# Delta rule and slot mixture: each head in its own 32 partitions, 32x32 diagonal products, layouts by VectorE block transposes

## Chip, core and metric

The kernel runs on one core of one Trainium2 chip. The metric is the device time of one execution in microseconds (us), the median of several runs. Everything is f32. The engines named here are TensorE (PE, with its weight loads as PEld), VectorE (DVE), ScalarE (ACT), GpSimd (POOL) and SyncE (SP, which only issues DMAs).

## The reference

Two blocks, one behind the other. The first is a delta rule over 768 tokens for 4 batch rows and 8 heads of 48 features; the second is a soft mixture of 8 experts with 4 slots each over the 3072 rows of 384 features that come out.

```python
# q, k, v: (4, 8, 768, 48); beta: (4, 8, 768)
k_n = k / (np.linalg.norm(k, axis=-1, keepdims=True) + 1e-06)
for t in range(S):
    y[:, :, t] = q_t @ state
    v_old = k_t @ state
    state = state + beta_t * outer(k_t, v_t - v_old)      # per batch row and head, 48 x 48
x = y.transpose(0, 2, 1, 3).reshape(3072, 384)
logits = x @ phi                                          # 3072 x 32 slots
d = softmax over the tokens; slot_input = d.T @ x         # 32 x 384
slot_out[e] = relu(slot_input[e] @ w1[e]) @ w2[e]         # 8 experts, 384 -> 1024 -> 384
out = softmax over the slots (logits) @ slot_out
```

## The kernel before

**Tiling.** Tokens are taken in 24 chunks of 32, and four chunks make a group (6 groups). A *unit* is one batch row b and one half g of the heads (4 heads), so that there are 8 units; in a unit, head h of the four and token t stand on partition 32 h + t. All 8 units of a chunk lie side by side in the free dimension.

**What does not depend on the state** is made for one group ahead. `norm` scales the keys (squares and scaling on POOL, the sum and a root with a correction step on DVE and ACT). `prep` brings K and Q of a chunk into `KQ` with features on partitions, by eight 128x128 PE transposes (L215) and two ACT copies (L218); then it forms K K^T and Q K^T by head, 48 rows by 32 columns (L230). ACT copies the first into `Lc` (L232). DVE spreads the second, masked, into `AT` (L233), where the four heads of a unit stand on the diagonal of a 128x128 matrix with zeros between them. `invert` forms the inverse of I + L of all four chunks at once: `Lc` goes to DRAM (`ld`, L250) and back as `lb` (L251), so that each partition holds one 32x32 block; POOL multiplies by beta (L252); then 31 elimination steps of two DVE instructions each (L264, L267) follow; the result goes to DRAM (`td`, L272). `near` fetches from there the inverse of the next chunk into the diagonal blocks of `TTs` (L282), and spreads the keys over the heads as `KX` on POOL (L291).

**One chunk** (`chunk`), with the state S: psR = K S (L310), R = V - psR on DVE (L314), psW = T R with a 128x128 matrix for each unit (L324), U = beta psW on DVE (L329), psS = K^T U (L340), S = S + psS on DVE (L345), psY = Q S + AT U (L354, and L359 with 128x128 matrices), and Y by ACT (L362). It goes by two halves of the batch rows, `hf`.

**Routing** (`route`) of a group follows one group later: logits (L379, L385), the two softmaxes, and the slots' inputs (L443, L453 on POOL, L458).

**The experts** (L532 on) come at the end, w1 as the stationary operand (L557), w2 as the moving one (L568), and then the output (L588).

**Order.** The code hands out steps of the work ahead and of the routing between the parts of a chunk (`Fill`, `merge`). A scheduler then orders each engine's queue by when it expects operands, so that the order on an engine is not the order of the code. Each engine takes its queue strictly in that order. An f32 product is two records of MATMUL and two of LDWEIGHTS in the trace (L340: 736 calls, x1472); a PE transpose is one of each.

Of the kernel before, what the change touches and what calls it, by code (L numbers as in the profile page):

```python
# [16 lines left out]
def kernel(  # L17
# [30 lines left out]
    DP = 64  # L48
# [5 lines left out]
    assert G == 2 and B == 4 and GC * U == C and Dm == H * D and NSL == C  # L54
# [5 lines left out]
    dp = ctx.enter_context(tc.tile_pool(name="dp", bufs=2, space=bass.MemoryType.DRAM))  # L60
# [8 lines left out]
    Ks = [io.tile([P, GC, U, DP], F32, name=f"Ks{i}", bufs=1) for i in range(2)]  # L69
    Qs = io.tile([P, GC, U, DP], F32, name="Qs", bufs=1)  # L70
    Vt = {}

    def load(src, dst, n, eng):
        for c in range(GC):
            for h in range(4):
                s0 = (n * GC + c) * C
                eng.dma_start(  # L77
                    out=dst[C * h:C * h + C, c, :, 0:D],
                    in_=src.rearrange("b (g h) s d -> h s (b g) d", h=4)[h, s0:s0 + C])

# [542 lines left out]
```

## Time and profile before

| | before |
|---|---|
| median of 3 runs | 921.85 us (921.1 to 922.2) |
| the profiled execution: its span | 919.5 us |
| TensorE busy | 679.9 us (74%) in 8324 matmuls |
| VectorE busy | 299.4 us (33%) |
| GpSimd busy | 192.9 us (21%) |
| ScalarE busy | 101.3 us (11%) |
| instructions | 19108 |

The span runs from the first to the last instruction of one execution; the run's time is 2.35 us longer. The busy share is an average over parts that differ: a start until the first inverse is there, six groups of chunks, the routing of the last group, and the experts. How each of them is bounded is read from the views below: the windows give busy time by stretch, the timeline gives single instructions with the idle time before them and what ended it, and the groups by line give counts and mean durations.

### The profile page before, as it was taken

The page shows a single profiled execution, that of the slowest core. Times are in us where ns is not written, and L with a number is a line of the kernel's source. Part 1 is how long each engine was busy: PE and PEld are TensorE (multiplying, and loading weights), DVE is VectorE, ACT ScalarE, POOL GpSimd, SP SyncE. Part 2 cuts the span into 40 slices and gives each one's busy share as a digit, 9 for nine tenths or more (in the row PEclk, how much of TensorE's full clock was granted, in tenths as well). Part 3 has the DMA queues.
Part 4 walks back from the last instruction along what each step waited for, and adds up shares of the span by engine and source line. Part 5 has one row for each costly group of instructions (what it writes and reads, how often), then busy time and mean ns, then how long its engine had stood idle before and what let it go on. Part 6 is the DMA issues. An engine that isn't in the chain of part 4 may idle for free.

```text
span 919.5 us, 19108 instructions
## 1 busy us (share of the span) xinstructions
PE 679.9 (74%) x8324; PEld 565.6 (62%) x8324; DVE 299.4 (33%) x816; ACT 101.3 (11%) x223; POOL 192.9 (21%) x347
## 2 busy tenths in 40 slices
PE   1706569069990799807998069996499799999998
PEld 1504569058880688706888058885398696765754
DVE  3267112942139421394213942226421100000011
ACT  0303000021120211102111021111000110000001
POOL 7231213131251213412134111351210200000000
PEclk9999999999995555755557555565555567667765
DMA  6240763023310242102321021000100099990013
GB/s 118 37 85 26 133 115 72 1 52 55 75 20 0 58 70 55 20 0 58 69 55 19 0 58 32 25 2 0 35 13 1 1 266 211 237 231 16 1 60 146
DMA packets 148019, 58.12 MB, mean 63 GB/s; under 512 B 131968, under 2 KB 143328, under 8 KB 147936
## 3 DMA queue, kind: packets, MB, share of 16 engines
q1 hardware_dynamic: 141888, 55.87, 27.9%
q10 hardware_dynamic: 5664, 0.94, 0.6%
q8 instruction: 65, 1.06, 0.5%
q0 software_dynamic: 384, 0.10, 0.1%
q14 instruction: 18, 0.15, 0.1%
HBM read 45.86 MB, written 11.01 MB: 62 GB/s over the span
## 4 chain that ended last, share of the span: by engine, by line
PE 64%; DVE 17%; DMA 6%; POOL 4%; SPq 3%; ACT 3%; issue 2%; ACTq 0%; DVEq 0%; POOLq 0%
PE ph L557 9%; PE psW L324 8%; PE psY L359 7%; DVE pr L264 7%; PE pso L568 6%; PE psS L340 6%; DVE tt L267 6%; PE pt L215 5%; PE pt L385 5%; PE pt L458 3%; PE pout L588 3%; PE psR L310 2%; PE pt L230 2%; PE psY L354 2%; PE pt L379 2%; SPq L77 2%
## 5 line engine op out<-in xcount | busy, mean ns | idle before, releaser
L215 PE MATMUL pt<-ident,Ks 128*128 128x128 f32 x96 | 42.1, 438 | 167.9 <-POOL Ks L199 158.7
L291 POOL TENSOR_TENSOR KX<-Ks,hm 128x192 f32<-128x192 f32 x184 | 91.0, 531 | 354.0 <-PE psS L340 264.4
L215 PEld LDWEIGHTS pt<-ident,Ks 128*128 128x128 f32 x96 | 20.8, 216 | 173.9 <-POOL Ks L199 159.6
L324 PE MATMUL psW<-R,TT 128*128 128x48 f32 x384 | 86.6, 396 | 34.4 <-DMA TT<-td 31.2
L324 PEld LDWEIGHTS psW<-R,TT 128*128 128x128 f32 x384 | 81.1, 311 | 39.4 <-DMA TT<-td 19.1
L557 PEld LDWEIGHTS ph<-sacc,w1t 96*128 96x128 f32 x512 | 87.8, 272 | 3.8 <-issue 3.8
L557 PE MATMUL ph<-sacc,w1t 96*128 96x4 f32 x512 | 88.1, 310 | 0.0
L359 PE MATMUL psY<-U,AT 128*128 128x48 f32 x384 | 83.9, 393 | 0.0
L264 DVE TENSOR_TENSOR pr<-tt,lb 128x31 f32<-128x31 f32 (+15 forms) x186 | 76.7, 413 | 16.2 <-POOL lb L252 11.0
L359 PEld LDWEIGHTS psY<-U,AT 128*128 128x128 f32 x384 | 78.2, 306 | 3.4
L267 DVE TENSOR_TENSOR tt<-tt,pr 128x31 f32<-128x31 f32 (+15 forms) x186 | 73.3, 394 | 5.2
L340 PE MATMUL psS<-U,KX 128*48 128x48 f32 x1472 | 69.8, 271 | 0.0
L340 PEld LDWEIGHTS psS<-U,KX 128*48 128x48 f32 x1472 | 60.8, 181 | 6.3 <-issue 1.7
L568 PE MATMUL pso<-w2t,hx 128*32 128x384 f32 x128 | 58.5, 627 | 1.7 <-DVE hx L561 1.7
L329 DVE TENSOR_TENSOR U<-psW,bta 128x192 f32<-128x192 f32 x48 | 17.2, 358 | 113.4 <-PE psW L324 113.4
L345 DVE TENSOR_TENSOR S<-S,psS 112x384 f32<-112x384 f32 x46 | 25.5, 554 | 87.6 <-PE psS L340 87.3
L233 DVE TENSOR_TENSOR AT<-pt,bdm 128x512 f32<-128x512 f32 x48 | 31.9, 688 | 62.1 <-ACT Lc L232 59.0
L385 PE MATMUL pt<-phi,yT 96*128 96x32 f32 x192 | 45.1, 398 | 6.0 <-ACT yT L381 5.1
L230 PE MATMUL pt<-KQ 48*32 48x64 f32 x1536 | 47.5, 310 | 1.9
L385 PEld LDWEIGHTS pt<-phi,yT 96*128 96x128 f32 x192 | 42.0, 323 | 10.5 <-ACT yT L381 9.1
L561 DVE TENSOR_SCALAR hx<-ph 128x32 f32<-128x32 f32 x8 | 1.5, 192 | 141.0 <-PE ph L557 141.0
L354 PE MATMUL psY<-S,KQ 48*32 48x48 f32 x1536 | 46.1, 265 | 0.1
(107 smaller groups left out, 698.9 us busy)
## 6 DMA issues: line engine op xcount, KB each, us to landing
w1t<-in_moe_w_dram SPq DMA_DIRECT2D x16, 768.0 KB
w2t<-in_moe_w_dram SPq DMA_DIRECT2D x8, 1536.0 KB
Ks<-in_k_dram SPq DMA_DIRECT2D x96, 48.0 KB
V<-in_v_dram SPq DMA_DIRECT2D x96, 48.0 KB
out_dram<-ob SPq DMA_DIRECT2D x24, 192.0 KB
Qs<-in_q_dram SPq DMA_DIRECT2D x80, 48.0 KB
ld<-Lc SPq DMA_DIRECT2D x24, 128.0 KB
lb<-ld SPq DMA_DIRECT2D x6, 512.0 KB
```

The lines of the kernel that those rows point to most:

```text
L215: nc.tensor.transpose(tp[:, i, a, :], src[:, c, b * G:(b + 1) * G, :].rearrange("p g d -> p (g d)"), ident)
L230: nc.tensor.matmul(pg[rh, b], lhsT=KQ[cc][r, b, 0, rh], rhs=KQ[cc][r, b, :, rh], start=True, stop=True, skip_group_check=True)
L264: nc.vector.tensor_tensor(prv, tt[:, 0:m, j:j + 1].broadcast_to([P, m, w]), lb[:, j, j + 1:C].unsqueeze(1).broadcast_to([P, m, w]), op=ALU ...
L267: nc.vector.tensor_tensor(tt[:, 0:m, j + 1:C], tt[:, 0:m, j + 1:C], prv, op=ALU.subtract)
L291: nc.gpsimd.tensor_tensor(KX[cc][:, g, b], kn[:, b].unsqueeze(1).broadcast_to([P, 4, D]), hm.unsqueeze(2).broadcast_to([P, 4, D]), op=ALU. ...
L324: nc.tensor.matmul(pw[:, i, g, :], lhsT=T[:, (2 * hf + i) * G + g].rearrange("p h t -> p (h t)"), rhs=Rs[hf][:, i, g, :], start=True, stop ...
L340: nc.tensor.matmul(psS[DP * g:DP * g + D, i, h, :], lhsT=kx[:, g, 2 * hf + i, h, :], rhs=Us[hf][:, i, g, :], start=True, stop=True, skip_g ...
L354: nc.tensor.matmul(py[C * h:C * h + C, b, :], lhsT=kq[r, b, 1, C * h:C * h + C], rhs=old[b // 2][r, b % 2, h, :], start=(b == 0), stop=Fal ...
L359: nc.tensor.matmul(py[:, b, :], lhsT=at[:, g, b].rearrange("p h t -> p (h t)"), rhs=Us[b // 2][:, b % 2, g, :], start=False, stop=True, sk ...
L385: nc.tensor.matmul(pl, lhsT=yT[:, h].rearrange("p c t -> p (c t)"), rhs=phi[:, h, :], start=(h == 0), stop=(h == 3))
L557: nc.tensor.matmul(st["ph"][:, t, :], lhsT=w1t[e][:, h, t * P:(t + 1) * P], rhs=sacc[:, h, sl], start=(h == 0), stop=(h == 3))
L568: nc.tensor.matmul(pso, lhsT=hx[:, e, t, :], rhs=w2t[e][:, t, :], start=(e == 0 and t == 0), stop=(e == E - 1 and t == NFC - 1))
```

## The change

Each head now keeps to its own 32 partitions in all products. The 48 features of a head are split into 32 and 16 (`a` = 0, 1), and each product with K, Q or the state is two accumulating products, whose operand rows, weights and output all lie in the 32 partitions of head h. So T, `AT` and K need no zeros between the heads: `TT`, `AT` and the keys are used as they are, as 32x32 blocks at the places (h, h) of the array.

- `KQ` comes from DVE block transposes (32x32 in place), four instructions a chunk, instead of eight PE transposes and two ACT copies. `Lc` to `lb` and `tt` to `TT` are DVE block transposes too; `ld`, `td`, `near`, `TTs` and `KX` are gone, and so are beta's second copy `bta` and its DMAs.
- beta goes into the inverse by one POOL multiply (`back`), so U is a plain ACT copy. The state is summed in PSUM over all chunks (`start` only at the first), so S is an ACT copy of it, where a DVE addition stood.
- K has three buffers and Q two (two and one before), and a group's loads are issued at the start of a group two ahead. The work ahead is handed out in the first chunk of a group (`prep`) and in the three others (`invert` and routing, a third each).

The code for the experts and the routing's arithmetic stay as they are.

```diff
-    Ks = [io.tile([P, GC, U, DP], F32, name=f"Ks{i}", bufs=1) for i in range(2)]
-    Qs = io.tile([P, GC, U, DP], F32, name="Qs", bufs=1)
+    Ks = [io.tile([P, W * D + DX], F32, name=f"Ks{i}", bufs=1) for i in range(3)]
+    Qs = [io.tile([P, W * D + DX], F32, name=f"Qs{i}", bufs=1) for i in range(2)]
...
+    def rows(h, a=0):
+        return slice(C * h, C * h + (C if a == 0 else D - C))
+    def feats(a):
+        return slice(0, C) if a == 0 else slice(C, D)
...
-        def transposes(bh):
...
-                    nc.tensor.transpose(
-                        tp[:, i, a, :],
-                        src[:, c, b * G:(b + 1) * G, :].rearrange("p g d -> p (g d)"), ident)
-            nc.scalar.activation(KQ[cc][:, 2 * bh:2 * bh + 2], tp, ACT.Copy)
+        def transposes(a):
...
+            for i, t in enumerate((Ks[n % 3], Qs[n % 2])):
+                o = c * U * D + C * a
+                src = t[:, o:o + U * D].rearrange("p (u d) -> p u d", d=D)[:, :, 0:C]
+                nc.vector.transpose(KQ[cc][:, :, a, i, :], src)
...
+            for i in range(UH):
+                for a in range(2):
+                    for h in range(4):
+                        kq = KQ[cc][rows(h, a), hf * UH + i, a]
+                        nc.tensor.matmul(pg[rows(h), i], lhsT=kq[:, 0, :], rhs=kq,
+                                         start=(a == 0), stop=(a == 1), skip_group_check=True)
...
-                AT[cc][:, g], pg[:, :, 1, :].unsqueeze(2).broadcast_to([P, B, 4, C]),
-                bdm.unsqueeze(1).broadcast_to([P, B, 4, C]), op=ALU.mult)
+                AT[cc][:, hf * UH:hf * UH + UH], pg[:, :, 1, :],
+                upper.unsqueeze(1).broadcast_to([P, UH, C]), op=ALU.mult)
...
-                nc.sync.dma_start(out=ld[r].rearrange("u s t -> s u t"), in_=lc[r])
-            nc.sync.dma_start(out=lb, in_=ld)
+            nc.vector.transpose(lb, Lc.pop(n).rearrange("p w t -> p t w"))
...
-        def store():
-            TTb[n] = dp.tile([P, C, C], F32, name="td", tag="td")
-            nc.sync.dma_start(out=TTb[n], in_=st["tt"])
...
+        def back():
+            tt = st["tt"]
+            nc.gpsimd.tensor_tensor(tt, tt, bb[:, n].unsqueeze(2).broadcast_to([P, C, C]),
+                                    op=ALU.mult)
+            TT[n] = wk.tile([P, W, C], F32, name="TT", tag="TT")
+            nc.vector.transpose(TT[n].rearrange("p w i -> p i w"), tt)
...
+        def residual(hf):
...
+            for i in range(UH):
+                for a in range(2):
+                    for h in range(4):
+                        nc.tensor.matmul(pr[rows(h), i, :], lhsT=kq[rows(h, a), hf * UH + i, a, 0],
+                                         rhs=old[hf][rows(h, a), a, i, :],
+                                         start=(a == 0), stop=(a == 1), skip_group_check=True)
+            Rs[hf] = wk.tile([P, UH, D], F32, name="R", tag=f"R{hf}", bufs=1)
+            nc.vector.tensor_tensor(Rs[hf], v_, pr, op=ALU.subtract)
+        def update(hf):
...
+                    nc.tensor.matmul(pw[rows(h), i, :], lhsT=T[rows(h), w0 + hf * UH + i, :],
+                                     rhs=Rs[hf][rows(h), i, :],
...
+            nc.scalar.activation(Us[hf], pw, ACT.Copy)
+        def state(hf):
+            for a in range(2):
+                for i in range(UH):
+                    for h in range(4):
+                        nc.tensor.matmul(psS[hf][rows(h, a), a, i, :],
+                                         lhsT=Kf[rows(h), w0 + hf * UH + i, feats(a)],
+                                         rhs=Us[hf][rows(h), i, :],
+                                         start=(cc == 0 and a == 0 and i == 0), stop=True,
...
+            nc.scalar.activation(St[hf], psS[hf], ACT.Copy)
...
+        for i in range(U):
+            for h in range(4):
+                nc.tensor.matmul(py[rows(h), i, :], lhsT=at[rows(h), i, :],
+                                 rhs=Us[i // UH][rows(h), i % UH, :],
...
-    NF = 5
+    NF = 4
...
-        cut_i, cut_r = len(inv) // 2, len(routing) // 2
+        cut_i, cut_r = len(inv) // 3, len(routing) // 3
+        if n + 2 < NG:
+            load_k(n + 2)
+            load_q(n + 2)
```

GpSimd's queue between two groups, before: `sq` and the scaling are `norm` of the group two ahead, `db` is routing, and `lb` opens the elimination.

```order
L399 TENSOR_TENSOR Call<-el,mx 128x128
L453 TENSOR_TENSOR db<-dr,hm 128x128 x16
L252 TENSOR_TENSOR lb<-lb,bb 128x1024
L185 TENSOR_TENSOR sq<-Ks_75 128x1536
L291 TENSOR_TENSOR KX<-Ks_76,hm 128x192 x8
L199 TENSOR_TENSOR Ks_75<-Ks_75,rn 128x32x48
```

The same stretch of GpSimd's queue now, from one norm to the next:

```order
L180 TENSOR_TENSOR sq<-Ks_73 128x1536
L194 TENSOR_TENSOR Ks_73<-Ks_73,rn 128x1536
L240 TENSOR_TENSOR lb<-lb,bb 128x1024
L376 TENSOR_TENSOR Call<-el,mx 128x128
L430 TENSOR_TENSOR db<-dr,hm 128x128 x16
L261 TENSOR_TENSOR tt<-tt,bb 128x1024
L245 MEMSET tt 128x1024
L246 MEMSET tt 128x32
L180 TENSOR_TENSOR sq<-Ks_74 128x1536
L194 TENSOR_TENSOR Ks_74<-Ks_74,rn 128x1536
```

The multiplication that opens the elimination stood behind the routing's 16 instructions and now stands ahead of them; the new multiplication of `tt` closes the elimination, and the next norm stands behind it.

VectorE's queue around the start of an elimination, before: `R` and `S` belong to the group's last chunk.

```order
L464 TENSOR_TENSOR sacc<-sacc,pt 96x128 x4
L329 TENSOR_TENSOR U<-psW,bta 128x192 x2
L345 TENSOR_TENSOR S<-S,psS 112x384 x2
L314 TENSOR_TENSOR R<-V,psR 128x2x48 x4
L264 TENSOR_TENSOR pr<-tt,lb 128x31
L267 TENSOR_TENSOR tt<-tt,pr 128x31
```

VectorE's queue in the middle of an elimination now:

```order
L253 TENSOR_TENSOR pr<-tt,lb 128x256
L256 TENSOR_TENSOR tt<-tt,pr 128x16x16
L290 TENSOR_TENSOR R<-V,psC 128x192
L253 TENSOR_TENSOR pr<-tt,lb 128x255
L256 TENSOR_TENSOR tt<-tt,pr 128x15x17
L290 TENSOR_TENSOR R<-V,psC 128x192
```

And at its end, with the norm and the first block transposes of the next group:

```order
L441 TENSOR_TENSOR sacc<-sacc,pt 96x128
L264 STREAM_TRANSPOSE TT<-tt 128x32x32
L290 TENSOR_TENSOR R<-V,psC 128x192 x2
L181 TENSOR_REDUCE ssq<-sq 128x32
L185 TENSOR_SCALAR ssq<-ssq 128x32
L209 STREAM_TRANSPOSE KQ<-Qs_76 128x8x32
L187 RECIPROCAL rn<-nrm 128x32
L188 TENSOR_TENSOR rn<-rn,ssq 128x32
L189 TENSOR_TENSOR nrm<-nrm,rn 128x32
L190 TENSOR_SCALAR nrm<-nrm 128x32
L191 RECIPROCAL rn<-nrm 128x32
L290 TENSOR_TENSOR R<-V,psC 128x192 x2
```

And ahead of the norm that belongs to the third group, once (the `R` are those of chunks 5, 6 and 7, counted from one):

```order
L253 TENSOR_TENSOR pr<-tt,lb 128x31
L256 TENSOR_TENSOR tt<-tt,pr 128x31
L264 STREAM_TRANSPOSE TT<-tt 128x32x32
L290 TENSOR_TENSOR R<-V,psC 128x192 x6
L181 TENSOR_REDUCE ssq<-sq 128x32
L185 TENSOR_SCALAR ssq<-ssq 128x32
```

The elimination followed all products of its group's chunks; now those of the chunks' residuals `R` and the routing stand between its steps, and the norm of the group behind follows once `TT` is written.

## Rows read from the trace of the kernel before

**Rows 1.** The page: span, and busy time of PE with its share and instructions.

```profile
span 919.5 us, 19108 instructions
...
PE 679.9 (74%) x8324; PEld 565.6 (62%) x8324; DVE 299.4 (33%) x816; ACT 101.3 (11%) x223; POOL 192.9 (21%) x347
```

**Rows 2.** Windows: from:to, length, busy time per engine, granted clock, DMA share, GB/s.

```profile
core 0: us, PE busy (x) PEld busy (x) DVE busy (x) ACT busy (x) POOL busy (x), PEclk, DMA share, GB/s
304.30:419.00 114.70, 81.84 (x1275) 72.52 (x1275) 48.82 (x132) 16.26 (x35) 30.32 (x54) 0.54 0.20 41
419.00:504.60 85.60, 82.17 (x1268) 72.99 (x1272) 20.86 (x66) 16.03 (x34) 21.90 (x45) 0.55 0.27 54
500.00:504.00 4.00, 3.96 (x122) 3.63 (x122) 1.44 (x4) 1.95 (x3) 0.87 (x1) 1.00 0.02 4
504.60:534.40 29.80, 0.28 (x25) 0.14 (x13) 28.01 (x68) 0.23 (x1) 8.42 (x10) 0.53 0.00 1
709.30:737.80 28.50, 21.58 (x104) 18.58 (x103) 5.08 (x25) 4.18 (x10) 7.41 (x18) 0.54 0.01 1
737.80:919.50 181.70, 175.76 (x706) 120.16 (x704) 8.83 (x21) 9.05 (x18) 0.57 (x1) 0.65 0.59 148
```

**Rows 3.** VectorE's timeline in an elimination: start, length, instruction, [idle before <-releaser].

```profile
504.64 1.29 DVE L264 TENSOR_TENSOR pr<-tt,lb 128x31 f32<-128x31 f32 x1
...
516.93 0.42 DVE L264 TENSOR_TENSOR pr<-tt,lb 128x256 f32<-128x256 f32 x1
...
531.63 2.81 DVE L267 TENSOR_TENSOR tt<-tt,pr 128x60 f32<-128x60 f32 x1
```

**Rows 4.** TensorE's waits: who for whom, total us, times, longest us.

```profile
PE pt L215 <- POOL Ks L199: 158.7, 6, 30.4
```

**Rows 5.** TensorE's timeline, matmuls, inside a chunk of the fourth group.

```profile
452.71 1.52 PE L340 MATMUL psS<-U,KX 128*48 128x48 f32 x32
454.17 3.65 PE L359 MATMUL psY<-U,AT 128*128 128x48 f32 x16
457.75 1.52 PE L340 MATMUL psS<-U,KX 128*48 128x48 f32 x32
459.20 0.60 PE L310 MATMUL psR<-S,KQ 48*32 48x48 f32 x32
459.73 0.85 PE L385 MATMUL pt<-phi,yT 96*128 96x32 f32 x3
```

**Rows 6.** The same, weight loads, the products of a chunk ahead.

```profile
446.84 0.88 PEld L230 LDWEIGHTS pt<-KQ 48*32 48x32 f32 x44 [0.34 <-ACT KQ L218]
```

**Rows 7.** TensorE's timeline, matmuls, in the stretch at the higher granted clock.

```profile
502.97 0.43 PE L310 MATMUL psR<-S,KQ 48*32 48x48 f32 x32
503.22 0.74 PE L354 MATMUL psY<-S,KQ 48*32 48x48 f32 x18
```

**Rows 8.** Groups by line: instruction, xcount, busy us, mean ns, idle before, releasers.

```profile
L264 DVE TENSOR_TENSOR pr<-tt,lb 128x31 f32<-128x31 f32 (+15 forms) x186 | 76.7, 413 | 16.2 <-POOL lb L252 11.0
L267 DVE TENSOR_TENSOR tt<-tt,pr 128x31 f32<-128x31 f32 (+15 forms) x186 | 73.3, 394 | 5.2
...
L314 DVE TENSOR_TENSOR R<-V,psR 128x96 f32<-128x96 f32 x96 | 20.9, 250 | 17.0 <-PE psR L310 15.9 <-DMA Ks<-in_k_dram 1.0
...
L329 DVE TENSOR_TENSOR U<-psW,bta 128x192 f32<-128x192 f32 x48 | 17.2, 358 | 113.4 <-PE psW L324 113.4
...
L186 DVE TENSOR_REDUCE ssq<-sq 128x32 f32<-128x1536 f32 x6 | 10.5, 1746 | 3.6 <-POOL sq L185 3.6
```

**Rows 9.** Timeline of the start: squares, norm, beta, last elimination step, first use.

```profile
13.80 2.75 POOL L185 TENSOR_TENSOR sq<-Ks 128x1536 f32<-128x1536 f32 x1
...
21.37 2.76 POOL L199 TENSOR_TENSOR Ks<-Ks,rn 128x1536 f32<-128x1536 f32 x1 [4.82 <-DVE rn L196]
...
51.19 1.91 POOL L252 TENSOR_TENSOR lb<-lb,bb 128x1024 f32<-128x1024 f32 x1 [23.21 <-DMA Ks<-in_k_dram]
...
88.94 0.22 DVE L267 TENSOR_TENSOR tt<-tt,pr 128x31 f32<-128x31 f32 x1
...
96.71 1.91 PE L324 MATMUL psW<-R,TT 128*128 128x48 f32 x8 [6.58 <-DMA TT<-td]
```

More of the change, by code (lines that the diff above doesn't have):

```diff
@@ L301, in chunk @@
[L301 to L318 removed]
+        kq, at, T = KQ.pop(cc), AT.pop(cc), TT[n]
@@ new lines, in chunk @@
+        for hf in range(2):
+            residual(hf)
+        py = ps.tile([P, U, D], F32, name="psY", tag="psY", bufs=2)
+        if cc:
+            for i in range(U):
+                for a in range(2):
+                    for h in range(4):
+                        nc.tensor.matmul(py[rows(h), i, :], lhsT=kq[rows(h, a), i, a, 1],
+                                         rhs=old[i // UH][rows(h, a), a, i % UH, :],
+                                         start=(i == 0 and a == 0), stop=False,
+                                         skip_group_check=True)
@@ L319, in chunk @@
         fill()
         for hf in range(2):
-            pw = ps.tile([P, 2, G, D], F32, name="psW", tag="psW")
-            for i in range(2):
-                for g in range(G):
-                    nc.tensor.matmul(
-                        pw[:, i, g, :],
-                        lhsT=T[:, (2 * hf + i) * G + g].rearrange("p h t -> p (h t)"),
-                        rhs=Rs[hf][:, i, g, :], start=True, stop=True, skip_group_check=True)
-            Ut = wk.tile([P, 2, G, D], F32, name="U", tag=f"U{hf}", bufs=1)
@@ L349, in chunk @@
-        for g in range(G):
-            r = slice(DP * g, DP * g + D)
-            py = ps.tile([P, B, D], F32, name="psY", tag="psY", bufs=2)
-            for b in range(B):
-                for h in range(4):
-                    nc.tensor.matmul(py[C * h:C * h + C, b, :],
-                                     lhsT=kq[r, b, 1, C * h:C * h + C],
-                                     rhs=old[b // 2][r, b % 2, h, :],
-                                     start=(b == 0), stop=False, skip_group_check=True)
-            for b in range(B):
-                nc.tensor.matmul(py[:, b, :], lhsT=at[:, g, b].rearrange("p h t -> p (h t)"),
-                                 rhs=Us[b // 2][:, b % 2, g, :],
-                                 start=False, stop=True, skip_group_check=True)
-            nc.scalar.activation(Yn[:, c, :, g * D:(g + 1) * D], py, ACT.Copy)
+                state(hf)
@@ L365 @@
+        fill()
+        for i in range(U):
+            for h in range(4):
+                nc.tensor.matmul(py[rows(h), i, :], lhsT=at[rows(h), i, :],
+                                 rhs=Us[i // UH][rows(h), i % UH, :],
+                                 start=(cc == 0 and i == 0), stop=True, skip_group_check=True)
+        nc.scalar.activation(Yn[:, c].rearrange("p b (g d) -> p (b g) d", d=D), py, ACT.Copy)
+        fill()
     Call = cpool.tile([P, NG, B, NSL], F32, name="Call")
@@ L492, in merge @@
         return [f for _, _, f in sorted(keyed, key=lambda x: x[:2])]
-    drain(norm(0), *(prep(0, c) for c in range(GC)), invert(0), near(0))
+    drain(norm(0), *(prep(0, c) for c in range(GC)), invert(0))
     load_k(1)
@@ L545 @@
     nc.gpsimd.memset(hx, 0.0)
[L546 removed]
+    pso = ps.tile([NSL, Dm], F32, name="pso", tag="psC", bufs=2)
     def first(e):
@@ L554, in product @@
             if t == 0:
-                st["ph"] = ps.tile([P, NFC, SPE], F32, name="ph", tag="psR", bufs=2)
+                st["ph"] = ps.tile([P, NFC, SPE], F32, name="ph", tag="psY", bufs=2)
             for h in range(4):
@@ L586 @@
             i = n * B + b
-            po = ps.tile([P, Dm], F32, name="pout", tag=("psR", "psY")[i % 2], bufs=2)
+            po = ps.tile([P, Dm], F32, name="pout", tag=("psC", "psY")[i % 2], bufs=2)
             nc.tensor.matmul(po, lhsT=cT[:, n, b, :], rhs=so, start=True, stop=True)
```

214 lines of the change are left out of this document (71 added, 143 removed).

## The prediction, made before the changed kernel ran

> **What bounds the kernel now.** The page first: TensorE is busy 679.9 of 919.5 us [rows 1]. That share is an average, so the windows come next, cut where the work changes [rows 2]. The groups of chunks repeat every 114.7 us, in two parts. For 85.6 us TensorE is busy 82.17: chunks, products ahead and routing. Then for 29.8 us it does nothing (0.28), while VectorE is busy 28.01. The timeline shows what VectorE does there: the elimination, as the last thing in its queue [rows 3]. The waits give the price: TensorE's next transposes waited 158.7 us in six waits for the scaled keys, 30.4 at most [rows 4], since the norm's small VectorE steps stand between the last elimination steps. Behind the last chunk come 28.5 us of routing and 181.7 us of experts [rows 2]; the change touches neither. So a gain can only come from TensorE's time per group, from passing the elimination beside it, and from the start.
>
> **The price of a product.** I take pitches (start to start). A pair (weight load and matmul) with 48x32 weights and 48 columns takes (459.73 - 459.20) / 32 = 16.6 ns, with 64 columns 0.88 / 44 = 20 ns [rows 5, 6]. The 128x48 weights take (454.17 - 452.71) / 32 = 45.6 ns, the 128x128 ones (457.75 - 454.17) / 16 = 224 ns [rows 5]. [...]
>
> **TensorE, part by part.** Before, a chunk needed 32 pairs at 224 ns, 64 at 45.6, 128 at 16.6 and 64 at 20: 7.2 + 2.9 + 2.1 + 1.3 = 13.5 us, beside its 8 transposes. Now all pairs are small: 128 (residual) + 128 (psY from S) + 64 (T R) + 128 (state) + 64 (AT U) = 512, and 128 for the products ahead. No row shows four 32x32 tiles on the diagonal. The nearest is the 48x32 form, whose four heads also write four different 32-column places, so 16.6 ns (20 for the products): 8.5 us a chunk and 2.6 us ahead, 11.1. [...] A chunk has also a chain: residual, subtract (0.36 [rows 8]), T R, copy, state, copy. Two halves alternate and psY fills the first wait, so 8.5 us stays TensorE's work.
> [...]
>
> **VectorE.** Away: the spread of AT to 512 wide and the addition of S. New: 16 block transposes of 256 elements a group and two of 1024. No row has one. A VectorE instruction of 256 elements took 0.42 us [rows 3]. By its element price it lies between 0.29 (1746 ns for 1536 [rows 8]) and 0.67 us (250 ns for 96). I take 0.42, and 1.2 for 1024. The elimination keeps 62 instructions: (76.7 + 73.3) / 6 = 25.0 us [rows 8], 27 with the pauses. KX leaves GpSimd, and four trips to DRAM leave the path.
>
> **A lap.** I count from the moment TT of one group is written to the next, along the queues of the order shown.
> (a) GpSimd clears tt and squares, VectorE sums and takes the root, GpSimd scales. At the start this chain took from 13.80 to 24.13, 10.3 us [rows 9]; with the clearing and two R's 12.
> (b) Six block transposes (2.5), then 512 product pairs at 20 ns (10.2) with some 260 pairs of a chunk between (4.3): 17.
> (c) Copy of Lc, block transpose (1.2), beta (1.91 [rows 9]), an R and a logit ahead: 5.
> (d) Elimination 27, routing on VectorE 5.1 (the stretch behind the last chunk [rows 2]), four R's 1.4, and about 3 for GpSimd's 16 db's, since a VectorE instruction beside a GpSimd one waits: 2.81 us for a step of 0.22 [rows 3, 9]. Sum 36.5. In it TensorE has routing (21.6 [rows 2]) and over two chunks, some 43 us with waits, of which VectorE meets the last slot products; I add 3.
> (e) beta into tt, block transpose, hops: 3.5.
> Together 77 us against 114.7. TensorE has 34 + 10.2 + 21.6 = 66 in it, so the two engines bind nearly alike.
>
> **The sum.** Start: keys scaled at 24.1, products to 37, lb ready at 41 (53.1 before). The elimination there took 36 us to 89.16 with the norm and products of the second group in it [rows 9]; 13 block transposes come in for wider AT's, so 37, and 3.5 for TT: 82, against 96.7. Second group, no routing yet: one chunk and the remaining products 10, (c) 4, elimination with R's 29.5, (e) 3.5: 47, to 129. Third: a lap, and six R's stand ahead of ssq, so the norm waits for two whole chunks (17 + 2, not 4): 92, to 221. Three laps: 452. Last group: four chunks with 21.6 of routing between them and some waits, 53: 505. Routing 28.5 and experts 181.7: 715 us of span. The span before is 919.5 and the median 921.85, so I add 2.4: 717, say **716 us**. What is late next: TensorE's routing and chunks beside the elimination, then the chain (a) to (c), in which VectorE mostly waits.
>
> **Rivals.**
> *TensorE is faster* (0.18): the tiles pass at 7.8 ns, by the clock or since loads pass under other heads' products. [...] Then laps are VectorE's: 12 + 10 + 5 + 36.5 + 3.5 = 67; start 76, 42, 74, 3 x 67, tail 33, 210, 2.4: **638**.
> *TensorE is slower, but not by halves* (0.12): 25 ns a pair, between 20 and 45.6. A lap is then TensorE's, 4 x 12.8 + 12.8 + 21.6 with waits 93; 84, 56, 110, 3 x 93, tail 66, 210, 2.4: **807**. Block transposes at 0.67 would add only some 3 us a lap.
> [...]
> *The four heads don't run side by side* (0.09), the slower side. Before, the four heads shared rows and differed in columns; now both differ, and all four write one PSUM tile. If that costs as much as the two-place row, 45.6 ns, then 24 chunks hold 14,976 pairs = 683 us of TensorE; with 27 at the start, five routings 108, 210 and 2.4 it is 1030, with some waits **1050**. It decides from some 36 ns a pair on: (922 - 716) / (807 - 716) x 8.4 + 16.6. Against it: the four heads do overlap in psR, all in one tile.
> [...]
> *It does nothing* (0.01): the elimination is left alone behind the chunks by waits that I don't see, and eats the gain.
>
> **How the numbers follow.** The forecast (laps of 72 to 84 us, so 690 to 750) has 0.60; the rivals as given. The range is to hold 8 in 10: it takes in the faster case and the 25 ns one, 625 to 810, and leaves out the serial one. Faster by over 0.2% (about what a measurement of this kernel can tell from no change): 0.60 + 0.18 + 0.12 = 0.90; slower 0.09; within 0.01.
>
> **What would show it.** In the profile after: pairs at 16 to 20 ns; the elimination's 62 instructions with R's and routing between them, TensorE busy beside them; a pitch of TT near 77 us, with (a) to (c) about 34 of it; first T R near 82 us; experts at 181.7 as before. Wrong if pairs take over 30 ns, if a block transpose takes over 1 us, if instruction supply stalls TensorE (its pairs rise from 8324 to some 15,600), or if VectorE waits long for the routing inside the elimination.

## The result, and the profile after

The changed kernel takes 778.7 us (median of 4 runs, 774.3 to 785.9) against 921.5 (median of 4) for the kernel before: a ratio of 0.847, 95% interval 0.842 to 0.851. The sign and the range held; the forecast of 716 was 63 us too low. The profiled execution has a span of 777.1 us, and all stretches below are of it. Of e4 and e11 below, the execution that was profiled was the slowest (720.3 and 795.2 us); it counts in their medians and not in their ratios.

The page of after (span, busy time, the queue that brings instructions, the chain that ended last):

```profile
span 777.1 us, 34471 instructions
...
PE 601.7 (77%) x16236; PEld 506.3 (65%) x16236; DVE 265.1 (34%) x777; ACT 105.8 (14%) x245; POOL 111.9 (14%) x159
...
q8 instruction: 127, 2.08, 1.2%
...
PE 74%; issue 12%; DMA 4%; SPq 4%; DVE 3%; POOL 2%; ACT 1%; ACTq 0%; POOLq 0%
```

Beside [rows 1], TensorE's instructions have doubled (8324 to 16,236 pairs of load and matmul) while its busy time fell by 78 us. New is the 12% "issue" in the chain: time in which the engine waited for nothing that the profile shows. Below, such an idle time of TensorE is called a stop.

The windows, cut where TT of a group is written (length, busy time, granted clock; columns as in [rows 2]):

```profile
81.00:135.00 54.00, 40.12 (x1942) 37.44 (x1946) 28.90 (x78) 8.51 (x22) 5.24 (x5) 0.59 0.10 20
135.00:255.00 120.00, 89.71 (x3012) 81.55 (x3001) 41.45 (x123) 16.74 (x40) 17.54 (x23) 0.53 0.21 38
255.00:337.00 82.00, 66.06 (x2550) 59.62 (x2550) 41.78 (x127) 17.12 (x39) 19.55 (x24) 0.69 0.10 19
337.00:421.00 84.00, 68.91 (x2680) 62.26 (x2682) 41.12 (x125) 17.24 (x39) 18.96 (x23) 0.66 0.15 27
504.00:566.00 62.00, 51.44 (x1842) 46.12 (x1842) 7.36 (x30) 10.64 (x25) 4.77 (x13) 0.61 0.02 4
566.00:595.00 29.00, 22.14 (x182) 19.41 (x181) 5.93 (x28) 4.19 (x9) 8.52 (x22) 0.65 0.00 1
595.00:777.00 182.00, 176.19 (x709) 121.50 (x706) 8.83 (x21) 9.18 (x18) 0.91 (x1) 0.65 0.59 147
```

The stretch of [rows 2] in which TensorE did 0.28 us of work in 29.8 is gone: the elimination passes beside products. The laps (from one TT to the next) are 53.4, 120.5, 81.8, 84.5 and 83.0 us, where 47, 92 and three times 77 were forecast. Routing (29) and experts (182) are as before.

What TensorE waits for from the first TT to the end of the last chunk (total us, times, longest), the first rows:

```profile
PE psY L321 <- issue: 25.6, 17, 2.5
PE psC L286 <- issue: 20.5, 17, 2.1
PE psC L296 <- DVE TT L264: 18.0, 2, 14.9
PE pt L221 <- issue: 12.9, 15, 2.1
```

The rows of that view with "issue" sum to 83 us, those with another engine to 20. With 384 us of running (the windows), TensorE is accounted for in 467 of the 485 us: from the first inverse on it waits for VectorE twice, 3.1 us for the first TT and 14.9 for the third, and hardly otherwise. How it stops is seen in its weight loads behind a long wait (start, length, instruction, count, [idle before]):

```profile
255.17 1.31 PEld L296 LDWEIGHTS psC<-R,TT 32*32 32x32 f32 x64 [15.15 <-DVE TT L264]
256.48 2.13 PEld L306 LDWEIGHTS psS<-U,Ks 32*32 32x32 f32 x128
258.55 0.79 PEld L335 LDWEIGHTS psY<-U,AT 32*32 32x32 f32 x60
260.91 0.11 PEld L335 LDWEIGHTS psY<-U,AT 32*32 32x32 f32 x2 [1.57 <-issue]
...
260.95 1.41 PEld L286 LDWEIGHTS psC<-S,KQ 32*32 32x32 f32 x122
264.64 0.11 PEld L286 LDWEIGHTS psC<-S,KQ 16*32 16x32 f32 x2 [2.27 <-issue]
...
264.68 2.39 PEld L321 LDWEIGHTS psY<-S,KQ 32*32 32x32 f32 x122
```

64 + 128 + 60 pairs run in 4.2 us, 16.5 ns each. That this is the prediction's price is chance: the first 64 pairs, at a granted clock of 0.50, take 20.5 ns, the last 60, at 0.96 to 1.00, 13. Then the engine stops, and from there on it gets 128 pairs and stops again: starts at 260.91 and 264.64, 3.73 us apart, although the 128 pairs take only 1.5 to 2.5 us. Over the 83 such intervals between 75 and 615 us the mean is 3.73 us, **29 ns a pair**. 128 pairs are 256 instructions. The page's queue q8 brought 2.08 MB in 127 packets of 16.4 KB; TensorE's 16,236 loads and as many matmuls are 32,472 instructions, 256 for each packet. (In the kernel before 16,648 came in 65 packets, in e1 14,336 in 56.) By these counts q8 brings TensorE's instructions, one packet to a block of 128 pairs, and I read TensorE's stops as waits for the next block.

### The profile page after: what moved, and what is told of

Read it like the earlier page. It is cut to its first block, busy times and chain, and to the rows that moved or that the text cites. A ratio compares the mean times of both kernels' runs of the same rounds, so it can differ in the third digit from the quotient of the medians.

```text
span 777.1 us, 34471 instructions
## 1 busy us (share of the span) xinstructions
PE 601.7 (77%) x16236; PEld 506.3 (65%) x16236; DVE 265.1 (34%) x777; ACT 105.8 (14%) x245; POOL 111.9 (14%) x159
## 3 DMA queue, kind: packets, MB, share of 16 engines
q8 instruction: 127, 2.08, 1.2%
## 4 chain that ended last, share of the span: by engine, by line
PE 74%; issue 12%; DMA 4%; SPq 4%; DVE 3%; POOL 2%; ACT 1%; ACTq 0%; POOLq 0%
PE ph L531 11%; PE pt L221 8%; PE psS L306 7%; PE pso L542 7%; PE psY L321 7%; PE psC L286 7%; PE pt L362 5%; PE psC L296 4%; SPq L84 4%; PE psY L335 4%; PE pout L562 4%; PE pt L435 4%; PE pt L356 3%; DMA w1t<-in_moe_w_dram 2%; DMA Qs<-in_q_dram 1%
## 5 line engine op out<-in xcount | busy, mean ns | idle before, releaser
L221 PE MATMUL pt<-KQ 16*32 16x64 f32 (+1 forms) x3072 | 83.8, 279 | 72.3 <-DVE KQ L209 54.2
L221 PEld LDWEIGHTS pt<-KQ 16*32 16x32 f32 (+1 forms) x3072 | 73.7, 148 | 78.4 <-issue 48.6
L321 PE MATMUL psY<-S,KQ 32*32 32x48 f32 (+1 forms) x2944 | 67.0, 260 | 25.6 <-issue 25.6
L321 PEld LDWEIGHTS psY<-S,KQ 16*32 16x32 f32 (+1 forms) x2944 | 59.7, 150 | 29.6 <-issue 29.5
L286 PE MATMUL psC<-S,KQ 32*32 32x48 f32 (+1 forms) x2944 | 60.6, 243 | 20.5 <-issue 20.5
L306 PE MATMUL psS<-U,Ks 32*16 32x48 f32 (+1 forms) x2944 | 65.3, 256 | 10.9 <-issue 10.8
L286 PEld LDWEIGHTS psC<-S,KQ 16*32 16x32 f32 (+1 forms) x2944 | 53.2, 137 | 26.7 <-issue 25.4
L306 PEld LDWEIGHTS psS<-U,Ks 32*16 32x16 f32 (+1 forms) x2944 | 56.3, 135 | 16.8 <-issue 15.5
L296 PE MATMUL psC<-R,TT 32*32 32x48 f32 x1472 | 39.6, 274 | 18.3 <-DVE TT L264 14.9
L430 POOL TENSOR_TENSOR db<-dr,hm 128x128 f32<-128x128 f32 x96 | 42.0, 471 | 56.0 <-ACT dr L425 35.7
```

Of the source, the lines that this page charges most:

```text
L221: nc.tensor.matmul(pg[rows(h), i], lhsT=kq[:, 0, :], rhs=kq, start=(a == 0), stop=(a == 1), skip_group_check=True)
L286: nc.tensor.matmul(pr[rows(h), i, :], lhsT=kq[rows(h, a), hf * UH + i, a, 0], rhs=old[hf][rows(h, a), a, i, :], start=(a == 0), stop=(a == ...
L296: nc.tensor.matmul(pw[rows(h), i, :], lhsT=T[rows(h), w0 + hf * UH + i, :], rhs=Rs[hf][rows(h), i, :], start=True, stop=True, skip_group_c ...
L306: nc.tensor.matmul(psS[hf][rows(h, a), a, i, :], lhsT=Kf[rows(h), w0 + hf * UH + i, feats(a)], rhs=Us[hf][rows(h), i, :], start=(cc == 0 a ...
L321: nc.tensor.matmul(py[rows(h), i, :], lhsT=kq[rows(h, a), i, a, 1], rhs=old[i // UH][rows(h, a), a, i % UH, :], start=(i == 0 and a == 0), ...
L430: nc.gpsimd.tensor_tensor(db[:, b], st["dr"][:, c, b].unsqueeze(1).broadcast_to([P, 4, NSL]), hm.unsqueeze(2).broadcast_to([P, 4, NSL]), o ...
```

## The experiments

Each line: the edit, pairs a chunk of the chain with its products, median, ratio to the kernel before with its interval.

| | edit | pairs | us | ratio |
|---|---|---|---|---|
| after | | 640 | 778.7 | 0.847 (0.842 to 0.851) |
| e2 | half the columns | 640 | 816.7 | 0.888 (0.883 to 0.893) |
| e3 | norm earlier | 640 | 793.3 | 0.862 (0.858 to 0.866) |
| e5 | half the elimination | 640 | 784.1 | 0.852 (0.850 to 0.855) |
| e8 | first tiles only | 384 | 718.3 | 0.778 (0.773 to 0.783) |
| e10 | e5 and e8 | 384 | 680.7 | 0.739 (0.737 to 0.742) |
| e4 | K and Q transposed by TensorE | 400 | 699.6 | 0.760 (0.758 to 0.762) |
| e6 | e4 and e3 | 400 | 697.6 | 0.758 (0.754 to 0.763) |
| e7 | e6, a group ahead, TensorE's order fixed | 400 | 713.1 | 0.773 (0.769 to 0.776) |
| e9 | e7, all orders fixed, norms and loads earlier | 400 | 650.6 | 0.707 (0.705 to 0.708) |
| e11 | the plan of e9 on the tiles of after | 640 | 786.1 | 0.853 (0.849 to 0.857) |

**e1: the price of a pair by itself** (one execution, 648.2 us, without the reference's computation). Seven stretches of 512 products (in bf16 1024), this one and its variants:

```diff
+    for i in range(N):
+        h = i % 4
+        nc.tensor.matmul(pA[rows(h), 0:48], lhsT=wA[rows(h), 0:32], rhs=wA[rows(h), 64:112],
+                         start=True, stop=True, skip_group_check=True)
```

> Only TensorE's part is measured, the reference's computation is left out: seven stretches of 512 products each (1024 loads and 1024 matmuls; in the sixth 1024 products in bf16, the same number of instructions), one form in each, with TensorE idle for about 20 us ahead of each stretch. Forms: (A) 32x32 tiles of four heads in turn, 48 columns; (B) the same with 24 columns; (C) with 128 columns; (D) all on one 32x32 tile, 48 columns; (E) 48 rows by 32 columns in four column places that share their rows; (F) as A in bf16; (G) the whole array, 48 columns. Theory 'supply' (TensorE gets its instructions in blocks of 256, one block in some 3.3 to 3.7 us, whatever they do): the first two blocks of a stretch run at the pitch of their form (A near 20 ns a pair at the lower clock, 12 to 14 at the higher), then there is a stop about every 128 pairs, and A, B, C and F each take 26 to 30 us for their 1024 pairs; D, E and G take 1024 times 45 to 50 ns at the lower clock (46 to 51 us) without stops, and show stops only where the higher clock brings a pair under 27 ns. Theory 'array' (a pair of four tiles side by side costs 20 to 28 ns of the array's own time, by its columns): no stops at regular places, B takes about half of A, C over twice A.

TensorE's weight loads (columns as above); L61 is A, L69 B, L77 C, L84 D, L92 E, L100 F, L107 G:

```profile
28.95 4.15 PEld L61 LDWEIGHTS pA<-wA 32*32 32x32 f32 x224 [28.95 <-DVE wA L43]
33.71 1.43 PEld L61 LDWEIGHTS pA<-wA 32*32 32x32 f32 x128 [0.60 <-issue]
37.16 1.43 PEld L61 LDWEIGHTS pA<-wA 32*32 32x32 f32 x128 [2.03 <-issue]
...
48.90 2.60 PEld L61 LDWEIGHTS pA<-wA 32*32 32x32 f32 x128 [2.57 <-issue]
52.90 2.60 PEld L61 LDWEIGHTS pA<-wA 32*32 32x32 f32 x128 [1.40 <-issue]
...
99.71 1.79 PEld L69 LDWEIGHTS pB<-wB 32*32 32x32 f32 x128 [2.21 <-issue]
103.71 1.80 PEld L69 LDWEIGHTS pB<-wB 32*32 32x32 f32 x128 [2.21 <-issue]
...
138.22 29.65 PEld L77 LDWEIGHTS pC<-wC 32*32 32x32 f32 x1024 [26.54 <-issue]
194.56 81.94 PEld L84 LDWEIGHTS pD<-wD 32*32 32x32 f32 x1024 [26.69 <-issue]
...
308.22 2.60 PEld L92 LDWEIGHTS pE<-wE 48*32 48x32 f32 x128 [0.60 <-issue]
...
365.65 1.33 PEld L100 LDWEIGHTS <-wF 32*32 32x32 bf16 x128 [2.67 <-issue]
...
411.34 218.53 PEld L107 LDWEIGHTS pG<-wG 128*128 128x128 f32 x1024 [26.09 <-issue]
```

and two windows of A (length, busy time of PE, PEld, VectorE, GpSimd, then the granted clock):

```profile
28.00:36.00 8.00, 5.84 (x351) 5.58 (x352) 0.90 (x1) 0.00 (x0) 1.00 0.02 4
48.00:57.00 9.00, 5.94 (x277) 5.58 (x280) 0.00 (x0) 0.00 (x0) 0.50 0.02 4
```

Inside a burst the four tiles side by side take 1.43 / 128 = 11.2 ns at a granted clock of 1.00, 20.3 ns at 0.50; at 0.50, 24 columns take 14.1 and bf16 10.4. But each of A, B, E and F needs 27.8 to 28.4 us for its 1024 pairs, 27 to 28 ns, with a stop behind every 128: blocks start 3.45 to 4.01 us apart, at 1.00 (A's first) as at 0.50. From rest 222 or 224 pairs run before the first stop. "Supply" holds for A, B and F, and "array" falls: B is no shorter than A. C, whose 29.7 us lie in the range of "supply", decides nothing: it never stops, because its own pitch, 29.65 us / 1024 = 29.0 ns (clock 0.94 from 138 to 168 us), is no shorter than the delivery. My figures for the long forms were wrong: E, 48 rows by 32 columns, runs like A (20.3 ns at 0.50); D, all on one tile, takes 80 ns, and G 213 (both at 0.50).

The trace also holds the start and length of each packet of q8. In A, B, E and F a block starts 1.2 to 1.6 us after a packet has ended, the next packet starts 1.0 to 1.7 us after the block's start, and it takes 0.9 to 1.5 us: together the 3.4 to 4.1 us of a block. No packet overlaps the one before it. I don't take loads of data for the cause: the DMA share is 0.02 here, and in after, where it is 0.11, the packets that follow one another within 4.4 us start 3.74 us apart as well (75 to 615 us).

**e2: half the columns, as many instructions** (so for all five products of the chain, the results used twice):

```diff
-                    nc.tensor.matmul(pw[rows(h), i, :], lhsT=T[rows(h), w0 + hf * UH + i, :],
-                                     rhs=Rs[hf][rows(h), i, :],
+                    nc.tensor.matmul(pw[rows(h), i, 0:HD], lhsT=T[rows(h), w0 + hf * UH + i, :],
+                                     rhs=Rs[hf][rows(h), i, 0:HD],
```

> The kernel after with every product of the chain (residual, update, state, reading of the state, AT times U) moving only 24 of its 48 columns; the results of the first 24 are used twice, so half of the value features are left out. As many instructions as before. Theory 'supply': a pair's price in long runs stays near 27 ns, so the time stays at 760 to 785 us. Theory 'array': 512 of a chunk's 640 pairs lose up to half of their 17 to 20 ns, 4 to 5 us a chunk over some 20 chunks, so 680 to 710 us.

From the first TT to the last chunk, after and e2:

```profile
81.00:566.00 485.00, 384.03 (x14567) 348.22 (x14568) 202.43 (x605) 87.35 (x203) 84.00 (x109) 0.62 0.11 21
```
```profile
82.00:610.00 528.00, 344.12 (x14574) 310.83 (x14575) 199.18 (x606) 86.73 (x203) 82.75 (x111) 0.53 0.10 19
```

TensorE runs 40 us less, although at a lower granted clock (0.53 against 0.62), and stops for issue 121 us instead of 83: the shorter pairs come back as stops, and the blocks still start 3.74 us apart (81 intervals). "Array" falls. The time rose by 38 us, outside both forecasts: waits for other engines went from 20 to 65 us, 45 of them for TT. In VectorE's queue the residuals stand at other places among the elimination's steps than in after; that this made the longer waits is likely and wasn't tried. It tells nothing of the pairs.

**e3: the norm earlier**, since in the third lap the norm's sum came 34 us behind its squares (136.05), after six residuals that each waited for TensorE. In VectorE's timeline of after:

```profile
139.39 0.35 DVE L290 TENSOR_TENSOR R<-V,psC 128x192 f32<-128x192 f32 x1 [4.77 <-PE psC L286]
...
154.71 0.35 DVE L290 TENSOR_TENSOR R<-V,psC 128x192 f32<-128x192 f32 x1 [12.51 <-PE psC L286]
...
170.34 0.35 DVE L290 TENSOR_TENSOR R<-V,psC 128x192 f32<-128x192 f32 x1 [12.29 <-PE psC L286]
172.79 0.35 DVE L290 TENSOR_TENSOR R<-V,psC 128x192 f32<-128x192 f32 x1 [2.09 <-PE psC L286]
173.07 1.74 DVE L181 TENSOR_REDUCE ssq<-sq 128x32 f32<-128x1536 f32 x1
```

```diff
-            if n + 2 < NG and c == 3:
+            if n + 2 < NG and c == 1:
                 drain(norm(n + 2))
...
+        if n + 3 < NG:
+            load_k(n + 3)
```

> The kernel after with a fourth buffer for K, K asked for one group earlier, and the norms of K written two chunks earlier in the program. On VectorE the norm of the third group then stands ahead of the six residuals that it waited behind (34 us from its squares to its sum), and from the fourth group on the norm is done a lap ahead. Theory 'queue order' (the third lap's 120 us and the 12 us at the head of each lap come from where the norm stands): the third lap falls to about 90 us, the fourth to the sixth by up to 10 us each, and the time to 720 to 750 us. Theory 'TensorE alone' (each lap is as long as its 2560 pairs and the routing take TensorE at 27 ns, 69 us and more, and the norm's place only changes where it idles): the third lap falls, but the later ones stay at 80 us, so 745 to 770 us. If the norm's place were of no account at all: 773 to 783 us.

The keys were scaled 33 us earlier (146.85 for 179.89), and the time rose by 15, outside all three forecasts: the third lap took 136 us, laps four and five 82 and 85 as before; the sixth fell to 69, but the last group rose from 62 to 72. TensorE, whose order now had four chunks of the chain ahead of the next group's products instead of three, went through them at 15 to 16 us each. "Queue order" falls for a kernel of 640 pairs; but as the new order also has a fourth chunk ahead, the run doesn't tell what the norm's place alone is worth.

**e5: half the elimination.**

```diff
         def eliminate(j):
+            if j % 2:
+                return
```

> The kernel after with every second step of the elimination left out (16 of 31 steps, so the inverse is incomplete); all else as it was. Theory 'chain' (as the prediction had it: a lap is the norm, the products, the transposition, the elimination and the inverse one behind the other, 77 us): each of the six laps gets about 17 us shorter, the time some 100 us, 665 to 690 us. Theory 'TensorE' (from the first inverse on, TensorE with its 128 pairs in 3.7 us sets every lap; in the trace of after it waits for another engine for only 20 us of the 485 between 81 and 566 us): the first inverse comes about 17 us earlier, at most the 15 us wait for the second and third are gone too, and the other laps stay at 80 to 85 us: 735 to 765 us.

The first inverse came 18 us earlier, and the kernel was not faster (784.1 us); laps four to six took 88 to 90 us instead of 82 to 85. In the fifth lap VectorE waited for the residuals' products 23.9 us (338 to 427 us), where after has 4.7 (337 to 421 us). "Chain" falls: the elimination did not set the laps. "TensorE" came nearer, but its laps of 80 to 85 and its 735 to 765 were wrong too: the early start was lost again in the third lap (132 us) and the laps behind it.

**e8: the number of products** (so also in the residual, the state and psY):

```diff
-                for a in range(2):
+                for a in range(1):
                     for h in range(4):
                         kq = KQ[cc][rows(h, a), hf * UH + i, a]
```

> The kernel after without the products of the second tile (the heads' features 32 to 47 are left out of the products, the residual, the state and the reading of the state): 384 pairs a chunk instead of 640, every remaining one as it was, the same 48 columns, the same block transposes, VectorE, ScalarE and GpSimd as before. It halves those products' instructions, where e2_half_columns halved their columns. Theory 'supply' (a pair costs the 27 to 31 ns of its delivery): 256 pairs a chunk are 7.4 us, 4 chunks a lap 30 us, until the laps end on the chain of norm, products and elimination (75 to 85 us from the fourth lap on is then no longer TensorE's): near the kernel with 400 pairs a chunk, 670 to 710 us. If instead the number of products were of no account (columns, clock or another engine): 760 to 780 us.

60 us less, a little above the range. The third lap took 96 us instead of 120 and the last group (the span less 211 us for routing and experts) 31 instead of 62, but laps four and five stayed at 84, and the sixth took 88. TensorE's longest wait is now (72 to 506 us; total us, times, longest):

```profile
PE psC L296 <- DVE TT L264: 58.8, 5, 16.3
```

There the ring takes over: TT, the residuals, norm, products, elimination, and TT again.

**e10: both.** The edits of e5 and e8.

> The edits of e5_half_steps and e8_first_part together: 16 of 31 elimination steps, and no products of the second tile (384 pairs a chunk). Alone, the first gave nothing (784.1 us) and the second 60 us, none of it in the fourth lap (83.9 us between two inverses). Theory 'both bind alike' (in a steady lap TensorE's pairs and the chain of norm, products and elimination each need some 80 us, so taking from one shows the other): with both shortened, the laps from the third on fall to 60 to 70 us and the time to 620 to 670 us. If a third thing held the lap (GpSimd, the loads, the written order): laps of 80 us again, 700 to 720 us.

680.7 us, between the two forecasts, and laps four to six were still 78 to 80 us, against "both bind alike". VectorE's queue holds them (its waits from 75 to 420 us):

```profile
DVE R L292 <- PE psC L288: 89.3, 22, 9.2
DVE AT L225 <- ACT Lc L224: 32.4, 36, 4.5
```

VectorE waits 89 us for residuals. In the fourth lap (202.3 to 282.5 us) six of them stand ahead of the norm's sum, 24 us from TT's end to it. So it takes 35 us until the keys are scaled, where after's fourth lap takes 14, and that uses up what the products (12 us for 24) and the elimination (26 for 36) give. These lengths are read from the trace; this kernel with its norm earlier was not run.

**e4 and e6: one part undone**, K and Q transposed by TensorE again, 48 rows in one tile; the inverse and its layouts as in after:

```diff
-                nc.vector.transpose(KQ[cc][:, :, a, i, :], src)
+                    nc.tensor.transpose(
+                        tp[:, i, a, :],
+                        src[:, c * U + b * G:c * U + (b + 1) * G, :].rearrange("p g d -> p (g d)"),
+                        ident)
+            nc.scalar.activation(KQ[cc][:, 2 * bh:2 * bh + 2], tp, ACT.Copy)
```

> The kernel after with the transposes of K and Q again by TensorE (eight whole-array transposes a chunk, copied by ScalarE) so that a head's 48 features lie on rows 64 g to 64 g + 47: the products, the residual and the reading of the state take one matmul of 48 rows by 32 columns where there were two of 32 and 16 rows, and the state one of 32 rows by 48 columns. 400 pairs a chunk instead of 640; the delta rule's inverse stays in 32x32 tiles and its layouts stay block transposes. Theory 'supply': 240 pairs fewer a chunk at 27 ns are 6.5 us, less about 1.5 us for changes of the array's mode and one wait for the state's banks: 5 us over 20 chunks, 100 us at most; the laps then end on the elimination (about 75 us each), so 680 to 730 us. Theory 'array' (the columns streamed set the price): a 48-row pair in two row places costs 23 ns and more at the lower clock against 2 times 17 to 20, the change of modes takes the rest back: 750 to 790 us.

699.6 us, in the range of "supply": the part that replaced TensorE's transposes of K and Q cost 79 us. It brought the second tile of 16 features with it and so 240 pairs a chunk; with 400 pairs TensorE's stops for issue are 15 us (81 to 520 us) instead of 83, and its wait for TT is 51 instead of 18. The time that both forecasts gave to changes of the array's mode was an estimate; no run shows such a cost by itself.

> Both together: the fewer pairs of e4_fewer_pairs and the early norms of e3_early_norm. In e4_fewer_pairs TensorE waits 51 us for the inverse, so there the chain of norm, products and elimination should end the laps. Theory: where the norms' place gave nothing with 640 pairs a chunk, it gives up to 10 us in each of three or four laps here: 660 to 690 us. If TensorE's array time (334 us of that stretch's 429) leaves no room: 695 to 705 us.

697.6 us: the norm's place is worth 2 us here at most (the runs overlap), not 10 to 40; its laps four and five still take 86 to 87 us, and only the sixth 54.

**e7, e9, e11: the ring opened.** The products two groups ahead, and the engines' instructions in the order written:

```diff
-                steps = [f for i in range(GC) for f in prep(n + 1, i)] if more else []
+            steps = merge(prep(n + 2, c) if n + 2 < NG else [], inv[i0:i1], routing[r0:r1])
...
+            return lambda *a, **k: tc.keep_in_program_order(getattr(self.engine, name)(*a, **k))
```

> As e6_fewer_early, and the transposes and products of a group done two groups ahead, a chunk of them in each chunk of the chain, with TensorE's instructions in the order in which they are written: the elimination of the next group can start when the last one's inverse is done, with nothing in front of it. If the lap was the chain of norm, products and elimination (82 to 88 us in e4_fewer_pairs), it falls to TensorE's 1600 pairs and the routing, some 60 to 65 us: 590 to 640 us. If waits in the written order (TensorE stops for each residual, update and state) make up for it: 660 to 700 us.

713.1 us, outside both forecasts: TensorE stood 87 us for the scaled keys, as its order no longer let it pass them.

> As e7_lap_ahead, with the instructions of all four engines in the order written and the loads of Q and the norms earlier; in e7_lap_ahead TensorE stood 87 us waiting for the scaling of K by the norm. If that wait was what took the gain back: 87 us less, less what becomes late next, 620 to 665 us. If the order written only moves the wait (to the residuals on VectorE behind elimination steps): 690 to 720 us.

650.6 us, the fastest of all. From its first TT to its last chunk, a lap, and the last group:

```profile
92.00:438.00 346.00, 268.82 (x9090) 226.71 (x9091) 189.82 (x529) 104.91 (x299) 76.45 (x111) 0.70 0.13 24
...
209.00:278.00 69.00, 52.10 (x1665) 44.00 (x1664) 40.37 (x111) 21.83 (x59) 17.43 (x23) 0.70 0.13 23
...
392.00:438.00 46.00, 39.24 (x1178) 32.95 (x1179) 7.19 (x30) 11.99 (x36) 6.28 (x17) 0.67 0.02 4
```

> The plan of e9_in_order (transposes and products two groups ahead, the written order on all engines, early loads and norms) on the tiles of the kernel after: 640 pairs a chunk. It tells the two limits of after apart. Theory 'delivery': with the ring through VectorE opened, a lap is still 2560 pairs at 27 to 29 ns, 69 to 75 us, and the routing's whole-array products behind them, 85 us or more, and the time stays at 740 to 790 us. Theory 'ring' (the engines' order of work alone made the laps 82 us and the pairs' number mattered only through it): laps of 63 to 69 us as in e9_in_order, 650 to 690 us.

786.1 us: with the same plan, 640 pairs a chunk instead of 400 are 135 us. Its laps three to five (in an execution with a span of 793.5 us) are 88 to 90 us. From its first TT to its last chunk:

```profile
104.00:582.00 478.00, 368.91 (x14404) 334.42 (x14405) 212.59 (x593) 83.97 (x197) 75.22 (x111) 0.64 0.10 18
```

Against e9 TensorE runs 100 us longer and stops for issue 46 us longer (65 against 19): 27.6 ns for each of the 5314 additional pairs, the price that e1 gives (27 to 28). "Delivery" holds; 47 us of waits for other engines remain in it. The two kernels differ in more than the count (TensorE's transposes, ScalarE's copies), so the 135 us are those of the form, not of the pairs alone.

## Why the prediction was right and wrong

**Where the 63 us are.** By the prediction's own sum:

| step | forecast | measured |
|---|---|---|
| first TT | 82 | 81.2 |
| second group | 47 | 53.4 |
| third lap | 92 | 120.5 |
| laps four to six | 3 x 77 | 81.8, 84.5, 83.0 |
| last group | 53 | 61.7 |
| routing and experts | 210.2 | 211 |

**The step that failed is the price of a product.** 16.6 ns was read from rows of 32 pairs [rows 5], behind 128-column products of 45.6 and 224 ns. The kernel before never asks for more than is delivered: its densest 8 us hold 266 pairs, 30 ns each, its densest 20 us 416, 48 ns each, and the list of its matmuls' waits has no row with "issue". In after's runs of hundreds of small pairs the sustained price is 27 to 29 ns by e1 and by after's own blocks, and fewer columns didn't lower it (B's 1024 pairs took 27.8 us for A's 28.4 in e1, and e2's blocks start 3.74 us apart). The prediction had named this ("if instruction supply stalls TensorE") as what would make it wrong, and put it at nothing in its sum. No row of the kernel before could give it a price, as none is a long run of small pairs.

The array's own price was too low as well, at the granted clock of its rows (0.50 from 452 to 460 us). The form of [rows 5] takes 20.3 ns in runs of 128 at 0.50 (e1 E), not 16.6. The products, with 64 columns, take 26.8 ns, not 20 (weight loads of after, clock 0.50 from 286.8 to 290.2 us):

```profile
286.83 3.43 PEld L221 LDWEIGHTS pt<-KQ 16*32 16x32 f32 x128 [2.29 <-issue]
```

That TensorE still runs only 66 to 69 us in laps four to six, as forecast (66), is in part luck: the granted clock was 0.65 to 0.69 there, and at 1.00 a pair took 11.2 ns where it took 20.3 at 0.50 (e1 A). What the forecast lacked in these laps is the stops.

TensorE then has some 80 us of work and stops in a lap, not 66. From 337 to 421 us the window gives 68.9 us of running, and the waits 16.6 us of stops in six rows and no other row.

**The chain's laps were nearly right, as a second limit.** In the lap from 255.2 to 336.9 us: (a) 14.0 for 12, (b) 24 for 17, (c) 3.8 for 5, (d) 36 for 39.5 with the 3 us added, (e) 3.9 for 3.5. The 7 us of (b) are TensorE's price again: the 779 pairs between 269.2 and 293.3 us pass at 31 ns, where 20 and 16.6 were taken. "The two engines bind nearly alike" was true at 82 us and not at 77: halving the elimination alone (e5) gains nothing, and cutting pairs alone (e8) nothing in laps four and five. Both together (e10) gain only 2 to 5 us in a lap, since the order of work on VectorE then holds it; the laps fell to 63 to 69 us only with fewer pairs and a fixed order (e9).

**The third lap** has 28.5 of the 63 us and was mis-sized twice. Three chunks, not two, ran ahead of the norm, and at 15.5 us (139.39 to 154.71 to 170.34), not 8.5. From TT to the scaled keys it took 48 us (134.6 to 182.7) where 27 were forecast. The 15.5 us are the price of a pair again: 512 pairs at 29 ns are 14.8. An earlier norm alone gained nothing (e3): TensorE had those chunks ahead of the products anyway.

**VectorE.** The block transposes of 256 elements took 415 and 412 ns, as taken (0.42); those of 1024 took 1.9 us, not 1.2. Groups by line of after:

```profile
L209 DVE STREAM_TRANSPOSE KQ<-Qs 128x256 f32<-128x256 f32 x48 | 18.6, 415 | 4.8 <-DMA Qs<-in_q_dram 4.8
...
L264 DVE STREAM_TRANSPOSE TT<-tt 128x1024 f32<-128x1024 f32 x6 | 11.5, 1917 | 10.9 <-POOL tt L261 10.9
L239 DVE STREAM_TRANSPOSE lb<-Lc 128x1024 f32<-128x1024 f32 x6 | 11.5, 1910 | 0.0
```

That is 1.4 us a lap in (c) and (e), within the other differences. The chain through VectorE, ScalarE and DRAM that the change removes did go, and with it the 29.8 us of [rows 2] in each group: TensorE's wait for the scaled keys, 158.7 us in [rows 4], has no row from 81 to 566 us.

**The rivals.** "Four heads don't run side by side" is refuted: 11.2 and 20.3 ns for four tiles in turn against 80 ns for one tile (e1 A and D), with all four in one PSUM tile. "TensorE is slower" had nearly the sustained price (25 for 27 to 29 ns), without its cause. No run shows 25 ns itself, an estimate between two rows: inside bursts a pair took 11.2 to 20.3 ns (e1 A), with 64 columns 26.8, and in long runs 27 to 29. The rival summed 93 us for a lap, where 82 to 85 were measured: it added waits to TensorE's time, and laps four to six have next to none beside the stops. "TensorE is faster" took 7.8 ns from two starts at a granted clock of 1.00 ((503.22 - 502.97) / 32 [rows 2, 7]); in runs of 128 a pair took 11.2 ns at that clock (e1 A). It is half true: the granted clock was 0.69 in the fourth lap against 0.53 in the third, and the pairs inside bursts were faster (13 for 20.5 ns behind 255 us), but the blocks came no faster: q8's packets that follow within 4.4 us start 3.78 us apart from 255 to 337 us, 3.76 from 135 to 255.

**What stays open.** In e1 a packet's own length varies by 0.6 us (0.9 to 1.5), the interval by as much (3.45 to 4.01); why 2.3 to 3.4 us pass between the end of one and the start of the next, the runs don't show. What holds e10's laps is read from its trace, not tried. Nor was the change taken apart the other way, its inverse and TT alone put into the kernel before; e4 is the nearest to it.

## What to carry to other kernels

Before a product is cut into small tiles, count the instructions: here TensorE got 256 of them (128 pairs) per 3.5 to 4 us, so in its long runs of small products pairs faster than 27 ns saved nothing (e1 A and B, e2), and where a product took two pairs for one, each pair more cost 27.6 ns (e11 against e9), and with 24 columns 27.2 for 27.7 with 48 (e1 B and A). A pitch read from a short burst was only a lower bound here (16.6 ns in rows of 32 pairs, 27 to 29 in long runs); read the price from a stretch that holds several hundred instructions of the same kind. Where two engines bind alike in a loop, a single edit can show nothing (e5, e8 in its laps four and five): shorten one and open the order of the other together (e9).

## What the runs showed of the hardware beyond that

- The interval between blocks was no shorter at the higher granted clock: 3.45 and 3.73 us at 1.00 (A's blocks from 33.71 to 40.89 us), 3.45 to 4.01 at 0.50 (e1).
- Each packet of q8 has 16,384 bytes, 256 of TensorE's instructions by the counts above (after: 32,472 in 127). None overlaps the one before it, and one takes 0.9 to 1.5 us of the 3.4 to 4.1 us between two starts in e1, and of 3.3 to 4.3 in after (75 to 615 us).
- From rest 222 to 252 pairs ran before the first stop (222 and 224 in e1, 252 in after behind 15.15 us of idle time at 255 us).
- Four tiles of 48 rows by 32 columns that share their rows ran like four diagonal tiles: both took 2.60 us for 128 pairs (e1 E and A at 0.50).
- A pair that follows on the same 32x32 place took 80 ns, four times the 20.3 ns of four places in turn (e1 D and A at 0.50).
- VectorE's 32x32 block transposes took 1.6 ns an element a partition at 256 elements and 1.9 at 1024 (415 and 1917 ns in after): no fixed part shows, though the two differ in layout too.
